# One order for all queues replaced by another, with 104 elementwise steps on other engines, in a fused attention and expert-layer kernel

## The chip, the cores and the metric

The kernel runs on one core of one Trainium2 chip. The core has a matrix engine (PE, with PEld for its weight loads), three elementwise engines (VectorE, called DVE here; ScalarE, called ACT; GpSimd, called POOL) and a queue that issues DMAs (SP). Each engine works through its own queue strictly in order and waits where an instruction needs another engine's result. The metric is the time in microseconds (us) of one execution on the device; lower is better. The kernel before takes 222.41 us (median of three runs, 222.18 to 222.57).

## What is computed

Clustered attention over 4 batches of 8 heads (768 tokens, 64 values a head): each query and each key is assigned to the nearest of 16 centroids, and a query attends only to keys of its own cluster. The result feeds a two-matrix layer with a softmax-weighted activation and a normalisation between the two matrices. Cut from the reference:

```python
q_assign = np.argmax(np.einsum('bhsd,hcd->bhsc', q_n, c_n), axis=-1)
k_assign = np.argmax(np.einsum('bhsd,hcd->bhsc', k_n, c_n), axis=-1)
mask = q_assign[:, :, :, None] == k_assign[:, :, None, :]
scores = np.where(mask, scale * q @ k.T, -1e9)
attn = softmax(scores);  x = attn @ v          # x: 3072 tokens x 512
h = x @ w_in                                   # 512 -> 1024
sm = softmax(h);  solu = h * sm
ln = (solu - mu) / np.sqrt(var + 1e-06) * g_ln
return ln @ w_out                              # 1024 -> 512
```

## The kernel before

The program is a list of some 1,570 named steps. Each step is added with its engine and the steps that it needs, and then a table, `ORDER`, says in which order all steps are written into the program. Since every engine has its own queue, the table sets the order of each queue and nothing else; a second table, `AWAY`, names steps that go to another engine than their usual one:

```python
def on(name, engine):
    return AWAY.get(name, engine)
...
for name in ORDER:
    o = self.ops[name]
    assert done.issuperset(o["first"]) and name not in done, name
    o["fn"]()
    done.add(name)
```

The steps that the change and the prediction speak of, by the first letters of their names:

- Loads on SP: `ld` (q and k of a pair of heads, into `raw`), `lv` (v), `lo` (w_out, 512 KB each), `li` (w_in, four parts of 512 KB into the three buffers `w_st`). A fourth part needs the first part's buffer back, that is, the cast `wi0` done. Behind them on the same queue come DMA transposes (`tx` of the attention's output x, `tu` of the activation u) and the stores `ou`.
- Preparation: `xa`, `xt` bring q and k, transposed, into `xt` (batch 0 through the matrix engine and a copy, L407 and L409; later batches by a DVE transpose, L421). `ca` casts a half of them to bf16 into `qbig` or `kbig` (L437 on ACT; L439 for q and L441 for k, with a scaling, on POOL or DVE). `cv` casts v (L554, L556). `cl`, `tb`, `mx`, `oh`, `ot` find the cluster of each token (matrix engine, then DVE). `pl` copies the cluster code under the q or k rows (L531), `bl` clears rows (L543).
- Attention: 144 regions. `S` is a half of a region's score products (L641), `E` its exponential on ACT (L651, 1024 columns), `V` the product with v (L663), six small matmuls each. 41 groups end in a normalisation `N` on DVE (L675 and L686). All `V` of a group write one bank, `ob`, so the next group's first `V` waits for `N`.
- The layer, in 24 tiles of 128 tokens: `h` products with w_in (L772), `hm` the maximum on DVE (L782), `ex` the exponential on ACT (L798), `u` the product of the two (L805, on DVE or POOL), `bn`, `ag` the statistics on DVE (L816, L821, L823), `as`, `al` small sums and a power (L835, L840), `y` products with w_out (L844), `sc` the scaling of the result (L856 on ACT, L858 on DVE).
- Once: `wi` casts w_in (L580, POOL), `mk`, `km` copy column sums (L611), `ce` centres w_out (L618 on DVE, L622 and L624 on POOL).

The score and v products of batch b run beside the layer tiles of batch b-1, so the matrix engine has two kinds of work to choose from after the first batch; in the first batch it has attention alone.

Of the kernel before, what the change touches and what calls it, by code (L numbers as in the profile page):

```python
# [38 lines left out]
lc ld0.0.0.0 ld0.0.1.0 ld0.0.0 ld0.0.1 ld0.1.0 ld0.1.1 lv0.0 ld0.2.0 ld0.2.1 ld0.3.0 lo3 lv0.1  # L39
ld0.3.1 lg lv0.2 lo1 lo2 lo0 cx z5 cy cz wu tp0.0.0.0 tp0.0.0.1 tp0.0.1.0 tp0.0.1.1 cp xa0.0.0  # L40
xt0.0.0 xa0.0.1 xt0.0.1 tp0.1.0.0 xa0.1.0 cb cl0.0 tb0.0 mx0.0 oh0.0 ot0.0 ca0.0.0.0.0 z3
ca0.0.1.0.0 ca0.0.0.0.1 cc ca0.0.0.1.1 ca0.0.0.1.0 pl0.0.1.1 pl0.0.0.0 ca0.0.1.0.1 ca0.0.1.1.1
ca0.0.1.1.0 tp0.1.0.1 tp0.1.1.0 xt0.1.0 xa0.1.1 cl0.0.1 tp0.1.1.1 cv0.0.1 xt0.1.1 pl0.0.0.1
tp0.2.0.0 tp0.2.0.1 tb0.0.1 mx0.0.1 oh0.0.1 ot0.0.1 pl0.0.1.0.1 pl0.0.1.0.0 pl0.0.1.1.1 cl0.1 sg
pl0.0.1.1.0 z1 ca0.1.1.0 cv0.0.0 ca0.1.0.0 xa0.2.0 pl0.0.1.0 tp0.2.1.0 xt0.2.0 xa0.2.1 S0.0 S0.1
E0 tp0.2.1.1 xt0.2.1 S1.0 tp0.3.0.0 S1.1 S2.0 S2.1 tp0.3.0.1 tb0.1 mx0.1 oh0.1 xa0.3.0 E1 E2 cl0.2
xt0.3.0 S3.0 S3.1 V0.0 V0.1 V1.0 S4.0 S4.1 V1.1 tp0.3.1.0 tb0.2 E3 S5.0 S5.1 E4 E5 ot0.1 N0 mx0.2
gt tp0.3.1.1 S6.0 S6.1 V2.0 V2.1 S7.0 S7.1 V3.0 V3.1 xa0.3.1 gk xt0.3.1 cl0.3 E6 E7 cv0.1.0
pl0.1.1.1 ca0.1.0.1 ca0.3.0.0 pl0.1.1.0 ca0.3.0.1 z2 ca0.1.1.1 oh0.2 pl0.1.0.0 pl0.1.0.1 gw S8.0
S8.1 S9.0 S9.1 me0 me1 ot0.2 tb0.3 pl0.2.1.0 N1 pl0.2.0.0 mx0.3 mk oh0.3 ca0.2.0.0 ca0.2.1.0  # L50
# [1304 lines left out]
```

## Time and profile before

| | us |
|---|---|
| median of three runs | 222.41 |
| span of the profiled execution | 220.5 |
| first exponential starts | 13.0 |
| first normalisation ends | 18.2 |
| thirty-first normalisation (`N30`) ends | 153.8 |
| last score region's exponential starts | 201.8 |

A span is the time from the first to the last instruction of the profiled execution. The view by stretches gives how long each engine was busy between two times, and in brackets how many instructions it ran; a matrix engine that shows as busy is not at its peak, since its matmuls overlap. A row of the groups gives engine, operation, output and inputs with their shapes, count, busy time, the mean of one in ns, and after the second bar the idle time of the engine just before such instructions, with what ended it.

### The profile page before, as it was taken

What the parts mean: (1) busy time and instruction counts of PE and PEld (TensorE: products, weight loads), DVE (VectorE), ACT (ScalarE), POOL (GpSimd) and SP (SyncE); (2) the same over time, 40 slices, a digit from 0 to 9 for tenths busy, and PEclk for the clock granted to TensorE, in tenths of its full rate; (3) what the DMA queues carried; (4) which work ended last, traced back from release to release, by engine and by line L of the source; (5) the groups of instructions that cost most, each with busy time, mean ns of one, the idle gap of its engine ahead of it and who ended that gap; (6) DMA issues with size and microseconds to landing.
All of it is one profiled execution on the core that took longest, in us unless ns stands there. A gap on an engine that the chain in (4) does not pass through costs nothing.

```text
span 220.5 us, 6292 instructions
## 1 busy us (share of the span) xinstructions
PE 211.4 (96%) x2401; PEld 148.9 (68%) x2431; DVE 185.7 (84%) x430; ACT 192.8 (87%) x245; POOL 158.8 (72%) x198
## 2 busy tenths in 40 slices
PE   7899999999999999999999999999999999999984
PEld 4567577677678776777677677666777767655442
DVE  3699979968999999896799999994888856989982
ACT  3799999999999998999999989999999888685362
POOL 3686969897898999549939997879889054456610
PEclk9999999999999999999999999999999999999999
DMA  5998999999999993999999981939584229777522
GB/s 199 394 402 259 189 175 300 126 154 259 164 154 169 190 188 62 174 248 210 153 225 162 180 184 38 171 92 209 151 173 90 72 64 168 154 120 170 163 94 100
DMA packets 120911, 38.33 MB, mean 174 GB/s; under 512 B 109993, under 2 KB 116401, under 8 KB 120881
## 3 DMA queue, kind: packets, MB, share of 16 engines
q1 hardware_dynamic: 120448, 37.40, 81.7%
q10 hardware_dynamic: 432, 0.52, 0.7%
q8 instruction: 19, 0.31, 0.6%
q14 instruction: 12, 0.09, 0.2%
HBM read 23.11 MB, written 6.29 MB: 133 GB/s over the span
## 4 chain that ended last, share of the span: by engine, by line
PE 72%; DVE 10%; DMA 6%; POOL 5%; issue 3%; ACT 2%; SPq 1%; DVEq 0%; ACTq 0%; POOLq 0%
PE sb L641 22%; PE hb L772 16%; PE mb L844 15%; PE ob L663 12%; DMA w_st<-in_moe_w_in_dram 4%; PE hb L470 3%; DMA raw<-in_q_dram 2%; DVE w_st L782 2%; PE hb L396 2%; DVE xt L421 2%; DVE bs L816 2%; POOL kbig L441 1%; PE mb L470 1%; POOL w_in_sb L580 1%; POOL v L556 1%
## 5 line engine op out<-in xcount | busy, mean ns | idle before, releaser
L651 ACT ACTIVATE e<-sb 128x1024 bf16<-128x1024 f32 x144 | 139.9, 1024 | 8.9 <-PE sb L641 8.1
L641 PE MATMUL sb<-qbig,kbig 80*128 80x256 bf16 (+3 forms) x648 | 83.8, 261 | 1.3 <-ACT e L651 1.0
L641 PEld LDWEIGHTS <-kbig 80*128 80x128 bf16 (+1 forms) x648 | 62.9, 119 | 25.4 <-issue 8.6
L805 POOL TENSOR_TENSOR u<-e_sb,w_st 128x1024 bf16<-128x1024 bf16 x21 | 45.1, 2145 | 20.0 <-ACT e_sb L798 13.3
L663 PEld LDWEIGHTS <-e 128*128 128x128 bf16 x1152 | 48.6, 97 | 10.4 <-DVE x L686 0.6
L663 PE MATMUL ob<-v,e 128*128 128x65 bf16 x1140 | 51.4, 193 | 0.2
L772 PE MATMUL hb<-w_in_sb,xT 128*128 128x512 bf16 x173 | 50.6, 379 | 0.9 <-POOL v L1323 0.3
L844 PE MATMUL mb<-w_out_c,uT 128*128 128x512 bf16 x165 | 45.5, 379 | 1.2 <-DVE y L858 0.4
L816 DVE BATCH_NORM_STATS2 bs<-u 128x6 f32<-128x512 bf16 x48 | 31.6, 680 | 1.1 <-POOL u L805 1.1
L798 ACT ACTIVATE e_sb<-w_st,nmax 128x1024 bf16<-128x1024 f32 (+1 forms) x25 | 27.8, 1113 | 3.2 <-DVE w_st L782 1.8
L439 POOL CAST qbig<-xt 64x768 bf16<-64x768 f32 (+1 forms) x31 | 25.7, 830 | 6.5 <-PE ob L663 2.7
L441 POOL TENSOR_SCALAR kbig<-xt 64x768 bf16<-64x768 f32 (+1 forms) x32 | 27.6, 865 | 2.4 <-DVE xt L409 0.8
L840 POOL TENSOR_TENSOR alpha<-var,halves 128x1 f32<-128x1 f32 x24 | 15.3, 638 | 12.6 <-DVE var L823 8.0
L421 DVE STREAM_TRANSPOSE xt<-raw 128x768 f32<-128x768 f32 x24 | 22.5, 959 | 0.1
L844 PEld LDWEIGHTS <-uT 128*128 128x128 bf16 x176 | 15.2, 97 | 10.2 <-issue 0.8
L772 PEld LDWEIGHTS <-xT 128*128 128x128 bf16 x192 | 15.8, 98 | 8.8 <-issue 0.6
L686 DVE TENSOR_TENSOR x<-ob,den 128x256 bf16<-128x256 f32 (+2 forms) x40 | 19.0, 474 | 1.4
L782 DVE TENSOR_SCALAR_CACHE_REDUCE w_st<-hb 128x512 f32<-128x512 f32 x24 | 16.3, 680 | 3.8 <-PE hb L772 3.7
L782 DVE TENSOR_SCALAR_CACHE_REDUCE w_st<-hb,nmax 128x512 f32<-128x512 f32 x24 | 17.8, 740 | 1.9 <-PE hb L772 1.5
L856 ACT ACTIVATE y<-mb,alpha 128x512 f32<-128x512 f32 x15 | 10.3, 685 | 6.5 <-POOL alpha L840 3.6
L675 DVE RECIPROCAL den<-ob 128x4 f32<-128x4 f32 (+2 forms) x40 | 7.1, 178 | 10.4 <-PE ob L663 10.1
L556 POOL CAST v<-vf 128x384 bf16<-128x384 f32 x22 | 10.9, 504 | 3.3 <-DMA vf<-in_v_dram 2.6
(109 smaller groups left out, 202.6 us busy)
## 6 DMA issues: line engine op xcount, KB each, us to landing
vf<-in_v_dram SPq DMA_DIRECT2D x16, 384.0 KB, 5.3
out_dram<-y SPq DMA_DIRECT2D x23, 256.0 KB, 2.5
raw<-in_k_dram SPq DMA_DIRECT2D x26, 192.0 KB, 4.6
raw<-in_q_dram SPq DMA_DIRECT2D x24, 192.0 KB, 5.1
w_g<-in_moe_w_out_dram SPq DMA_DIRECT2D x4, 512.0 KB, 8.7
w_st<-in_moe_w_in_dram SPq DMA_DIRECT2D x4, 512.0 KB, 8.0
raw<-in_q_dram SPq DMA_DIRECT2D x3, 384.0 KB, 6.6
raw<-in_k_dram SPq DMA_DIRECT2D x3, 384.0 KB, 7.6
```

The lines of the kernel that those rows point to most:

```text
L421: nc.vector.transpose(xts[b, p, i][:], raw_of(b, p, i))
L439: (nc.vector if e == "DVE" else nc.gpsimd).tensor_copy(dst, src)
L441: (nc.vector if e == "DVE" else nc.gpsimd).tensor_scalar(dst, src, scalar1=inv_C, scalar2=1.0, op0=Alu.mult, op1=Alu.mult)
L641: nc.tensor.matmul(reg[:, c:c + wd], kb[u, pp, side_of(h), keys], qb[u, pp, side_of(h), su * P:su * P + wd])
L651: nc.scalar.activation(es[r][:, :w], src, Act.Exp, scale=exp_scale, bias=-exp_scale)
L663: nc.tensor.matmul(ops_of(group_of[n])[:, s, :VW], es[r][:, c0:c0 + P], v1[index[b, pair_of(h)] % R][:, side_of(h), kt, :VW], start=(kt == ...
L772: nc.tensor.matmul(hb[f2][:], xTs[f][:, dc, :], w_in_sb[:, dc, f2 * BANK:(f2 + 1) * BANK], start=(dc == 0), stop=(dc == n_dc - 1))
L782: nc.vector.tensor_scalar(ff[f, "h"][:, f2 * BANK:(f2 + 1) * BANK], hb[f2][:], scalar1=-1.0, scalar2=nmax[:, f2 - 1:f2] if f2 else 3.0e38, ...
L798: nc.scalar.activation(ff[f, "e"][:, cols(f, f2)], ff[f, "h"][:, cols(f, f2)], Act.Exp, bias=ff[f, "nmax"][:, n_ff2 - 1:], scale=-1.0, acc ...
L805: (nc.vector if e == "DVE" else nc.gpsimd).tensor_tensor(ff[f, "u"][:, cols(f, f2)], ff[f, "e"][:, cols(f, f2)], ff[f, "h"][:, cols(f, f2) ...
L816: nc.vector.bn_stats(ff[f, "bs"][:, f2, :], ff[f, "u"][:, f2 * BANK:(f2 + 1) * BANK])
L844: nc.tensor.matmul(y_of(f, x), ff[f, "uT"][:, fc, :], w_out_c[:, fc, parts_of(f, x)], start=(fc == 0), stop=(fc == n_fc - 1))
```

## The change

Both tables are written anew. The operations, the buffers and what each step computes are the same. 104 of the 1,570 steps change engine, and nearly every queue has another order:

| steps | from | to | count |
|---|---|---|---|
| `ca` casts of q and k | POOL (16), ACT (1) | DVE | 17 |
| `ca` | ACT | POOL | 3 |
| `ca` | POOL | ACT | 1 |
| `cv` casts of v | ACT | POOL | 8 |
| `cv` | POOL | ACT | 4 |
| `cv` | POOL, ACT | DVE | 2 |
| `pl` copies | DVE | POOL | 12 |
| `pl` | POOL (5), ACT (2) | DVE | 7 |
| `pl` | ACT | POOL | 2 |
| `u` products | POOL | DVE | 6 |
| `u` | DVE | POOL | 2 |
| `sc` scalings | ACT to DVE 5, DVE to ACT 5 | | 10 |
| `as` sums | POOL to DVE 9, DVE to POOL 8 | | 17 |
| `ce` centrings | DVE to POOL 4, POOL to DVE 1 | | 5 |
| `xa`, `xt` copies | ACT to DVE 3, DVE to ACT 2 | | 5 |
| `bl` clears | POOL to DVE 2, DVE to POOL 1 | | 3 |

Steps by engine: DVE 301 before and 319 now, ACT 219 and 206, POOL 183 and 178; PE 722 and SP 143 in both. No `ca` stood on DVE before. The two tables together are two lines shorter, so a line of the kernel below it has a number that is smaller by 2.

```diff
 AWAY.update(dict.fromkeys("""
-    as0 as11 as14 as15 as17 as18 as19 as2 as22 as23 as4 as5 as9 bl1.2 bl3.0 ce0 ce2 ce4 km mk
...
+    as1 as10 as13 as15 as16 as17 as18 as19 as20 as21 as3 as5 as7 as8 bl1.0 bl2.0 bl3.0 ca0.0.0.0.1
+    ca0.1.0.1 ca0.3.0.0 ca1.0.0.0 ca1.0.1.1 ca1.1.0.0 ca1.1.0.1 ca1.1.1.0 ca2.1.0.0 ca2.1.0.1
+    ca2.1.1.0 ca2.2.0.0 ca2.2.1.1 ca2.3.0.1 ca3.1.0.1 ca3.2.0.1 ca3.3.0.0 ce0 cv0.2.1 cv0.3.1 km mk
...
 """.split(), "DVE"))
...
 ORDER = """
-lc ld0.0.0.0 ld0.0.1.0 ld0.0.0 ld0.0.1 ld0.1.0 ld0.1.1 lv0.0 ld0.2.0 ld0.2.1 ld0.3.0 lo3 lv0.1
...
+lc cx ld0.0.0.0 wu ld0.0.1.0 tp0.0.0.0 ld0.0.0 xa0.0.0 cy cz tp0.0.0.1 cp tp0.0.1.0 ld0.0.1 ld0.1.0
```

Three places show the moves. The first is the DVE queue around the normalisations `N6` to `N8` (each is a RECIPROCAL of `den` and the product into `x`). Before:

```order
L421 STREAM_TRANSPOSE xt<-raw 128x768 x2
L675 RECIPROCAL den<-ob 128x4
L686 TENSOR_TENSOR x<-ob,den 128x2x2x64
L479 STREAM_TRANSPOSE cst<-hb_92 128x384
L479 STREAM_TRANSPOSE cst<-hb_93 128x384
L489 TENSOR_REDUCE mx<-cst 128x48
L675 RECIPROCAL den<-ob 128x4
L686 TENSOR_TENSOR x<-ob,den 128x2x2x64
L493 TENSOR_TENSOR oh<-cst,mx 128x768
L782 TENSOR_SCALAR w_st,nmax<-hb_92 128x512
```

and now:

```order
L419 STREAM_TRANSPOSE xt<-raw 128x768
L731 COPY xT<-hb_93 128x1024
L439 TENSOR_SCALAR kbig_101<-xt 64x768
L673 RECIPROCAL den<-ob 128x4
L684 TENSOR_TENSOR x<-ob,den 128x2x2x64
L477 STREAM_TRANSPOSE cst<-hb_92 128x384
L477 STREAM_TRANSPOSE cst<-hb_93 128x384
L487 TENSOR_REDUCE mx<-cst 128x48
L437 CAST qbig_98<-xt 64x768
L673 RECIPROCAL den<-ob 128x4
L684 TENSOR_TENSOR x<-ob,den 128x2x2x64
L491 TENSOR_TENSOR oh<-cst,mx 128x768
```

Two casts now stand between normalisations on DVE, and the maximum of the layer's first tile (L782) comes later.

The second is the POOL queue where w_in is cast (the CAST into `w_in_sb` is `wi`; the pairs of operations on `w_g` are `ce`). Before:

```order
L556 CAST v_3_105<-vf 128x6x64 x2
L580 CAST w_in_sb<-w_st 128x1024
L622 TENSOR_SCALAR w_g<-w_g,g_ln_111 128x512
L624 TENSOR_TENSOR w_out_c<-w_g,y 128x512
L622 TENSOR_SCALAR w_g<-w_g,g_ln_111 128x512
L624 TENSOR_TENSOR w_out_c<-w_g,y 128x512
L441 TENSOR_SCALAR kbig_101<-xt 64x768
L580 CAST w_in_sb<-w_st 128x1024 x3
```

and now:

```order
L554 CAST v_3_105<-vf 128x6x64
L437 CAST qbig_98<-xt 64x768
L620 TENSOR_SCALAR w_g<-w_g,g_ln_111 128x512
L622 TENSOR_TENSOR w_out_c<-w_g,y 128x512
L620 TENSOR_SCALAR w_g<-w_g,g_ln_111 128x512
L622 TENSOR_TENSOR w_out_c<-w_g,y 128x512
L578 CAST w_in_sb<-w_st 128x1024 x3
L1321 MEMSET v_4_106 128x12x2
L578 CAST w_in_sb<-w_st 128x1024
```

The first cast of w_in, which frees the buffer for the fourth load, now stands behind both centrings.

The third is the SP queue where w_in is loaded. Before:

```order
L596 DMA w_g<-in_moe_w_out_dram 128x2x512 x3
L413 DMA raw<-in_q_dram 32x48x32
L574 DMA w_st<-in_moe_w_in_dram 128x1024
L413 DMA raw<-in_q_dram 32x48x32 x3
L413 DMA raw<-in_k_dram 32x48x32
L548 DMA vf<-in_v_dram 128x2x384
L413 DMA raw<-in_k_dram 32x48x32 x3
L574 DMA w_st<-in_moe_w_in_dram 128x1024 x3
L413 DMA raw<-in_q_dram 32x48x32 x4
```

and now:

```order
L411 DMA raw<-in_q_dram 32x48x32 x2
L594 DMA w_g<-in_moe_w_out_dram 128x2x512
L546 DMA vf<-in_v_dram 128x2x384
L411 DMA raw<-in_q_dram 32x48x32 x2
L546 DMA vf<-in_v_dram 128x2x384
L411 DMA raw<-in_k_dram 32x48x32 x4
L572 DMA w_st<-in_moe_w_in_dram 128x1024 x4
L546 DMA vf<-in_v_dram 128x2x384
L411 DMA raw<-in_q_dram 32x48x32 x4
```

All four loads of w_in now stand in a row behind the first eight small loads of batch 1, and the loads behind them (v and the next q and k) wait while the fourth waits for its buffer.

More of the change, by code (lines that the diff above doesn't have):

```diff
@@ new lines @@
+V71.0 S109.1 V71.1 E108 y6.1 u10.0 S110.0 S110.1 tb3.2 E109 h12.0.0 hm11.1 N29 S111.0 E110 as9
+bn9.0 xt3.3.0 y6.2 S111.1 xt3.3.1 V72.0 ou4 V72.1 S112.0 h12.0.1 hm12.0 E111 S112.1 y6.3 ca3.1.1.1
+al6 as10 cv3.1.1 V73.0 V73.1 E112 S113.0 ag8 lv3.3 S113.1 tu8 cl3.3 ex11.0 ou5 E113 tb3.3 S114.0
+S114.1 E114 V74.0 h12.1.0 ca3.3.1.1 tx14 sc6 bn9.1 h12.1.1 S115.0 S115.1 tu9 V74.1 y7.0 S116.0
+mx3.2 u11.0 h13.0.0 N30 S116.1 E115 hm12.1 oh3.2 E116 bn10.0 V75.0 h13.0.1 S117.0 V75.1 V76.0 ot3.2
+S117.1 bn10.1 h13.1.0 S118.0 as11 ex12.0 E117 y7.1 V76.1 S118.1 V77.0 hm13.0 y7.2 V77.1 h13.1.1
```

212 lines of the change are left out of this document (101 added, 111 removed).

## The prediction

> **What bounds the kernel now.** I read the page's busy times first, then the view by stretches.
>
> ```profile
> span 220.5 us, 6292 instructions
> PE 211.4 (96%) x2401; PEld 148.9 (68%) x2431; DVE 185.7 (84%) x430; ACT 192.8 (87%) x245; POOL 158.8 (72%) x198
> ```
>
> Four engines lie between 72% and 96%, so an average decides nothing; the stretches do. Columns: the stretch, its length, busy time and instructions of each engine, granted clock, DMA share, GB/s.
>
> ```profile
> 20.00:45.00 25.00, 23.59 (x319) 16.25 (x318) 21.62 (x43) 24.36 (x29) 20.03 (x26) 1.00 0.99 193
> 45.00:90.00 45.00, 44.26 (x557) 33.66 (x562) 42.36 (x88) 43.65 (x52) 40.33 (x44) 1.00 0.97 170
> 90.00:150.00 60.00, 59.41 (x703) 43.66 (x712) 54.73 (x117) 57.64 (x72) 46.20 (x52) 1.00 0.90 166
> 150.00:200.00 50.00, 49.52 (x571) 34.47 (x576) 38.29 (x101) 42.49 (x55) 30.33 (x30) 1.00 0.67 134
> 18.20:153.80 135.60, 132.86 (x1628) 97.93 (x1647) 121.83 (x256) 131.21 (x158) 111.81 (x127) 1.00 0.96 176
> ```
>
> From 45 us on PE is busy 98.4 to 99.0% of the time: it is the bound, and no order of the other queues can make it shorter there. Only in 20 to 45 us does it fall to 94%, and there ACT is the full engine (24.36 of 25). So what the change can win lies ahead of 45 us, and what it can lose lies anywhere. The clock was 1.00 throughout. The waits of PE and DVE agree; the second row is from the waits of 18 to 154 us alone, as is the third:
>
> ```profile
> PE sb L641 <- ACT e L651: 1.0, 3, 0.3
> DVE den L675 <- PE ob L663: 4.7, 9, 1.3
> DVE w_st L782 <- PE hb L772: 4.1, 5, 2.5
> ```
>
> DVE is early at the normalisations and maxima: in that stretch it waited 8.8 us for PE, and PE hardly for it.
>
> **The change, part by part.** I take the stretch in which nearly all moved steps fall, from the end of the first normalisation to the end of the thirty-first (`N30`), and what comes before and behind it.
>
> ```profile
> 17.74 0.42 DVE L686 TENSOR_TENSOR x<-ob,den 128x256 bf16<-128x256 f32 x1
> 153.29 0.56 DVE L686 TENSOR_TENSOR x<-ob,den 128x384 bf16<-128x384 f32 x1
> ```
>
> These two end at 18.2 and 153.8 us, which is the fifth stretch above: 135.6 us.
>
> *PE's side.* Counted in the two orders, PE has between the first `V` behind `N0` and the first behind `N30` the same score and v products, but 53 halves of `h` steps instead of 60 and 29 quarters of `y` steps instead of 39: the layer is put off. A step of these has two matmuls of 512 columns, and the chain gives four in 0.87 and 0.86 us:
>
> ```profile
> 56.97 0.87 PE hb L772 x4
> 87.99 0.86 PE mb L844 x4
> ```
>
> 17 steps at 0.43 us are 7.3 us of PE that leave the stretch and are done behind it. At PE's own pace of before the stretch would take 135.6 - 7.3 = 128.3 us.
>
> *DVE's side.* The same count gives what DVE gains between these normalisations: 14 casts (0 before), 2 casts of v, 1 clear, 2 scalings, 1 product `u`, 1 small sum. It loses 1 `ag`, 1 `bn`, 3 `ce`, 4 `hm`, 1 `mx` and 2 `oh` (one of each in batch 0), 2 `pl` (one in batch 0) and 1 copy into `xt`. The rows:
>
> ```profile
> L531 DVE COPY qbig<-oht 32x768 f32<-32x768 f32 x7 | 4.9, 702 | 0.2
> L531 DVE COPY kbig<-oht 32x768 f32<-32x768 f32 x2 | 1.7, 867 | 0.0
> L556 POOL CAST v<-vf 128x384 bf16<-128x384 f32 x22 | 10.9, 504 | 3.3 <-DMA vf<-in_v_dram 2.6
> L858 DVE TENSOR_SCALAR y<-mb,alpha 128x512 f32<-128x512 f32 x8 | 5.9, 736 | 1.8 <-POOL alpha L840 1.2 <-PE mb L844 0.7
> L805 DVE TENSOR_TENSOR u<-e_sb,w_st 128x1024 bf16<-128x1024 bf16 x2 | 2.4, 1222 | 0.0
> L543 DVE MEMSET kbig<- 16x768 f32 x2 | 1.4, 698 | 0.4 <-issue 0.4
> L816 DVE BATCH_NORM_STATS2 bs<-u 128x6 f32<-128x512 bf16 x48 | 31.6, 680 | 1.1 <-POOL u L805 1.1
> L618 DVE SCALAR_TENSOR_TENSOR w_out_c<-w_g,g_ln,y 128x512 bf16<-128x512 f32 x5 | 4.1, 830 | 0.0
> L782 DVE TENSOR_SCALAR_CACHE_REDUCE w_st<-hb,nmax 128x512 f32<-128x512 f32 x24 | 17.8, 740 | 1.9 <-PE hb L772 1.5
> L493 DVE TENSOR_TENSOR oh<-cst,mx 128x768 bf16<-128x768 f32 x6 | 7.2, 1206 | 0.0
> ```
>
> No cast of q or k on DVE is in the trace. The nearest work is the copy of `pl`, as many elements a row from memory to memory: the nine copies of the first two rows average (7 x 0.702 + 2 x 0.867) / 9 = 0.74 us. They hold two kinds, as the view of that line shows (min/median/max in ns):
>
> ```profile
> L531 DVE COPY qbig<-oht x13: 351/552/1164, 12.1 to 160.6; 32x768 f32<-32x768 f32 x7, 32x384 f32<-32x384 f32 x4, 32x192 f32<-32x192 f32 x2
> L441 POOL TENSOR_SCALAR kbig<-xt x32: 505/827/1612, 6.9 to 152.2; 64x768 bf16<-64x768 f32 x29, 64x384 bf16<-64x384 f32 x3
> 23.59 1.01 DVE L531 COPY qbig<-oht 32x384 f32<-32x384 f32 x1
> 22.66 2.64 POOL L441 TENSOR_SCALAR kbig<-xt 64x768 bf16<-64x768 f32 x3
> ```
>
> 0.55 us is a copy left alone and 1.16 us one that met work on POOL; the copy of 23.59 us, half as long, took 1.01 us while POOL was casting. So a cast costs 0.55 to 1.16 us, and I take 0.74, the mean of what copies met here. Added: 14 x 0.74 + 2 x 0.50 + 0.70 + 2 x 0.74 + 1.22 + 0.15 = 14.9 us (the clear and the small sum at the 0.70 and 0.15 us that they take on DVE before). Removed: 0.47 + 0.68 + 3 x 0.83 + 4 x 0.71 + 0.55 + 1.81 + 1.26 + 0.55 = 10.7 us (`hm` at the mean of its two forms; batch 0's `mx`, `pl` and copy at 0.55 to 0.56 and its `oh` at 0.60, half of a later one's size). DVE's busy time in the stretch becomes 121.8 + 4.2 = 126.0 us. Before, it was idle 135.6 - 121.8 = 13.8 us, of which 8.8 us on PE and 0.2 us on the cluster product vanish if DVE is the late one; 4.8 us in small gaps and waits for POOL stay. **DVE needs 126.0 + 4.8 = 130.8 us where PE needs 128.3.** DVE becomes the bound: every `N` comes late, the next group's first `V` waits for it on PE, and the scores, exponentials and layer products queued behind that `V` wait too. That is +2.5 us, and what PE loses there it cannot win back, as it is full behind it.
>
> *ACT's side.* From 13 to 60 us ACT was full:
>
> ```profile
> 13.00:60.00 47.00, 45.47 (x599) 32.91 (x600) 41.49 (x86) 46.20 (x55) 38.53 (x50) 1.00 0.99 218
> ```
>
> Seven elementwise steps leave its queue between exponentials there (`xa`, `xt`, two `cv`, a `pl`, two `ca`) and one copy comes: 0.48 + 0.48 + 0.51 + 0.51 + 0.51 + 0.84 + 0.84 - 0.48 = 3.7 us (0.48 from the copies, 0.51 the v casts and the copy of `pl`, 0.84 the casts on ACT). While DVE sets the pace this buys nothing; it is what rival 1 lives on.
>
> *The start.* The chain to the first score product is as long as before (transposes, cluster product, then five steps on DVE and the copies): the one-hot turn stands behind one more small transpose (0.36 us) and DVE does one copy (0.45 us) that ACT did. Between 0 and +0.4 us, covered until `N0` by PE's transposes; I take 0.
>
> *w_in.* The chain that ends last runs here before through the loads, in order of time:
>
> ```profile
> 32.66 1.00 POOL w_in_sb L580
> 33.68 7.99 DMA w_st<-in_moe_w_in_dram
> 41.72 1.04 POOL w_in_sb L580
> 42.81 0.38 PE L772 MATMUL hb<-w_in_sb,xT 128*128 128x512 bf16 x1 [0.33 <-POOL v L1323]
> ```
>
> A buffer is freed at 33.7 us, the fourth part lands 8 us later, is cast, and PE waited 0.33 us. Now the freeing cast stands behind the centring of two parts, and that behind `km`. The rows for it (the last is the four loads' time to landing):
>
> ```profile
> 29.83 0.42 DVE L686 TENSOR_TENSOR x<-ob,den 128x256 bf16<-128x256 f32 x1
> 30.17 0.68 DVE L611 COPY y<-hb 128x512 f32<-128x512 f32 x1
> L421 DVE STREAM_TRANSPOSE xt<-raw 128x768 f32<-128x768 f32 x24 | 22.5, 959 | 0.1
> L622 POOL TENSOR_SCALAR w_g<-w_g,g_ln 128x512 f32<-128x512 f32 x3 | 2.5, 841 | 0.1
> L624 POOL TENSOR_TENSOR w_out_c<-w_g,y 128x512 bf16<-128x512 f32 x3 | 3.8, 1277 | 0.3
> DMA to landing us min/median/max: 5.2/8.0/10.5
> ```
>
> By the clock of before the fourth normalisation ends at 30.3 us; then a cast of v (0.50), `mk` (0.68), a transpose (0.96), a normalisation (0.60), a cast (0.50) and `km` (0.68) end on DVE at about 34.2; two centrings on POOL (0.84 + 1.28 us each) end at 38.4, the first cast of w_in at 39.4. With 5.2 us to the median of 8.0 us for landing, the fourth part is cast at 45.6 to 48.4. PE comes to that product 15 steps later, 3.1 us (8 half regions of 0.22 and 7 `V` of 0.19 us), at 45.9. The wait is -0.3 to +2.5 us (+5.0 at the longest landing); SP's queue has nothing else in flight while it waits, which speaks for the short landing. A late DVE also brings PE there later, so most of it is covered: I take 0.5. Queued behind the fourth load are v and the next q and k of batch 1, needed by DVE only some 10 us later.
>
> *Behind `N30`.* PE has 7.3 us more to do and remains the bound at its 99%; DVE (38.3 of 50 us busy) has room. 0, at most +1.
>
> **Sum.** 130.8 - 128.3 + 0 + 0.5 + 0 = +3.0 us on the profiled span of 220.5, so 223.5; the median stands 1.9 us above the span, and the same addition gives 225.4 us.
>
> The rule that bears on the price of a cast is in the Trainium skill, SBUF — State Buffer, section Who interferes with whom: DVE casts and scalings that use both port pairs and any POOL instruction exclude each other, and whichever comes second is blocked for the whole of the first. The trace agrees in kind: 1.01 us for the short copy beside POOL's casts.
>
> **Rivals.** POOL's longest steps stand behind the second of them:
>
> ```profile
> L805 POOL TENSOR_TENSOR u<-e_sb,w_st 128x1024 bf16<-128x1024 bf16 x21 | 45.1, 2145 | 20.0 <-ACT e_sb L798 13.3 <-issue 5.6 <-DVE y L858 0.6
> ```
>
> 1. *The gain (other side).* The casts run alone, at 0.55: 14 x 0.19 = 2.7 us less, so DVE is busy 123.3 us. If its gaps as the late engine are those of ACT in 13 to 60 us (0.8 of 47, so 2.3 us in the stretch), it needs 125.6, below 128.3, and ACT's 3.7 us let PE follow. Then -2.7 us: 219.7. For it: POOL is less loaded, and ACT shows how few gaps the late engine leaves. Against it: by their mean, some three in ten of the copies met POOL ((0.74 - 0.55) / (1.16 - 0.55)). It decides once DVE's need falls below 128.3 us.
> 2. *Blocked casts.* POOL is busy 82% of the stretch (111.8 of 135.6). If every cast waits for what POOL has under way, half of an instruction weighted by length (45 of POOL's 159 us at 2.14 and the rest at some 0.82 us: (0.28 x 2.14 + 0.72 x 0.82) / 2 = 0.60), it costs 0.55 + 0.82 x 0.60 = 1.04 us: 14 x 0.30 = 4.2 us more, 229.6. For it: single copies took 1.16. Against it: they averaged 0.74. By the rule of the Trainium skill above, this is the case in which DVE is always the second to come.
> 3. *w_in decides.* The fourth part lands after 8 us and nothing covers it: +2.0 on the sum, 227.4.
> 4. *Nothing lost, nothing won.* Casts at 0.55 and gaps of 4.8 us: 128.1 against PE's 128.3, and 222.4.
>
> **Numbers.** Forecast 0.46, rival 1 0.24, rival 2 0.15, rival 3 0.08, rival 4 0.07. Slower by over 0.2% (0.44 us, about what three runs of this kernel can tell): 0.46 + 0.15 + 0.08 = 0.69; same 0.07; faster 0.24. Predicted 225.4 us. The forecast's own range is 223.0 to 227.5; the 8-in-10 range cuts the better half of rival 1 off, and goes past rival 2 by what casts of 1.16 us would add (14 x 0.12 = 1.7): 219.8 to 231.3.
>
> **What would show it.** Right: in 20 to 150 us DVE busy above 95%, idle hardly ever for PE at L673 and L780, PE below 97% with waits for the normalisation at the `V` products; casts on DVE of 0.55 to 1.2 us; ACT with idle time ahead of its exponentials. Wrong: PE at 98% from 30 us on and DVE still waiting for it (rival 1), or a stall of PE of over 2 us near 46 us and none later (rival 3). A stall in a place that I have not counted, above all behind 150 us, would make the sum wrong whichever sign it has.

## The result, and the profile after

| | us |
|---|---|
| before, median of 4 runs beside it | 222.3 (221.92 to 222.57) |
| changed, median of 4 runs | 235.67 (234.33 to 237.10) |
| ratio, 95% interval | 1.061 (1.056 to 1.066) |
| span of the profiled execution | 233.5, before 220.5 |

The change costs 13.4 us where 3.0 were forecast. The sign is the forecast's; the time lies above its range. Of the 10.0 us between the span forecast (223.5) and the one measured (233.5), 0.4 lie ahead of `N0`, 7.4 between `N0` and `N30` (with the forecast's 0.5 us for w_in counted there) and 2.2 behind.

The changed kernel's page, first line and busy times of the engines:

```profile
span 233.5 us, 6302 instructions
PE 217.4 (93%) x2399; PEld 148.3 (64%) x2431; DVE 204.0 (87%) x447; ACT 187.7 (80%) x232; POOL 153.6 (66%) x197
```

The same stretches as before the change (columns as there: length, busy time of PE, PEld, DVE, ACT and POOL, granted clock, DMA share, GB/s); the last runs again from the end of `N0` to the end of `N30`:

```profile
20.00:45.00 25.00, 23.63 (x325) 15.79 (x324) 22.03 (x44) 22.15 (x24) 20.78 (x29) 1.00 0.95 227
45.00:90.00 45.00, 44.03 (x529) 31.94 (x535) 43.33 (x87) 41.75 (x49) 39.03 (x42) 1.00 0.97 166
90.00:150.00 60.00, 55.11 (x648) 40.01 (x655) 55.66 (x112) 51.17 (x61) 42.97 (x48) 0.98 0.89 168
150.00:200.00 50.00, 48.27 (x553) 33.79 (x561) 40.85 (x95) 42.32 (x54) 20.81 (x26) 0.99 0.37 85
18.58:157.28 138.70, 131.20 (x1589) 93.61 (x1608) 127.88 (x257) 122.22 (x140) 107.83 (x123) 0.99 0.89 172
```

Up to 45 us nothing is lost: PE is busy 23.6 us of 25 as before, and `N7` ends at 40.5 us where it ended at 42.7. ACT, full there before, has nearly 3 us of 25 free. From `N0` to `N30` it takes 138.7 us where 130.8 were forecast. DVE is busy 127.9 us of them, close to the 126.0 of the sum, but idle 10.8 us, not 4.8. It still waits for PE, as the waits of that stretch show (who waits for whom: us in total, times, longest), while PE waits for it once for long:

```profile
PE hb L770 <- DVE cst L477: 2.8, 1, 2.8
DVE cst L477 <- PE hb L468: 2.6, 5, 1.1
DVE den L673 <- PE ob L661: 2.6, 4, 0.9
DVE w_st L780 <- PE hb L770: 0.7, 1, 0.7
```

So DVE is not what sets the pace all along, though the forecast had it so. It is late in single places. The largest one, in the timeline of 143 to 148 us (start, duration, engine and line, what ended the idle time before it):

```profile
142.91 0.83 POOL L439 TENSOR_SCALAR kbig<-xt 64x768 bf16<-64x768 f32 x1
143.69 3.23 DVE L803 TENSOR_TENSOR u<-e_sb,w_st 128x1024 bf16<-128x1024 bf16 x1 [0.86 <-DMA uT<-u]
143.71 2.13 POOL L803 TENSOR_TENSOR u<-e_sb,w_st 128x1024 bf16<-128x1024 bf16 x1
145.92 1.05 POOL L833 TENSOR_SCALAR es<-esum 128x1 f32<-128x1 f32 x1
146.84 0.57 DVE L477 STREAM_TRANSPOSE cst<-hb 128x384 f32<-128x384 f32 x1
147.47 0.59 PE L770 MATMUL hb<-w_in_sb,xT 128*128 128x512 bf16 x2 [2.80 <-DVE cst L477]
```

The first `u` on DVE (`u10`) starts just before POOL's cast ends, runs on beside POOL's `u9` and takes 3.23 us instead of the 1.22 of a lone one. Behind it in DVE's queue stands `tb3.2` (the transpose into `cst`), which empties the bank `hb` that the layer product `h12.0.0` needs; PE stands for 2.80 us. Then the clock falls (stretches of 2.5 us, columns as above):

```profile
145.00:147.50 2.50, 0.03 (x1) 0.03 (x1) 2.50 (x3) 0.79 (x1) 2.33 (x3) 1.00 1.20 302
147.50:150.00 2.50, 2.50 (x16) 1.51 (x16) 2.47 (x6) 0.14 (x1) 1.39 (x3) 0.59 0.50 116
150.00:152.50 2.50, 2.28 (x28) 1.64 (x27) 1.82 (x6) 1.48 (x2) 0.83 (x1) 0.73 0.00 0
152.50:155.00 2.50, 2.50 (x29) 1.40 (x26) 1.37 (x4) 2.50 (x5) 0.80 (x1) 1.00 0.54 105
```

At 0.59 and 0.73 of full speed, 5 us of PE lose some 2.5 x 0.41 + 2.5 x 0.27 = 1.7 us more, by estimate. Two smaller cases of the same kind lie behind 150 us. At 164 us a copy of the cluster code on DVE (`pl3.2.1.1`) takes 2.12 us beside POOL's `u12`, and the maximum queued behind it holds a layer product up for 1.03 us:

```profile
164.11 2.14 POOL L803 TENSOR_TENSOR u<-e_sb,w_st 128x1024 bf16<-128x1024 bf16 x1
164.56 2.12 DVE L529 COPY kbig<-oht 32x768 f32<-32x768 f32 x1
...
168.47 0.59 PE L770 MATMUL hb<-w_in_sb,xT 128*128 128x512 bf16 x2 [1.03 <-DVE w_st L780]
```

At 199 us it is `u17` beside `u18`, and a maximum queued behind it holds PE up for 0.91 us:

```profile
198.51 2.15 POOL L803 TENSOR_TENSOR u<-e_sb,w_st 128x1024 bf16<-128x1024 bf16 x1 [1.87 <-DMA uT<-u]
...
199.06 2.67 DVE L803 TENSOR_TENSOR u<-e_sb,w_st 128x1024 bf16<-128x1024 bf16 x1
...
202.40 1.02 PE L770 MATMUL hb<-w_in_sb,xT 128*128 128x512 bf16 x4 [0.91 <-DVE w_st L780]
```

The groups of the whole execution (busy time, mean ns of one, idle time before them) show that the casts cost what was forecast, and what the layer products waited for:

```profile
L437 DVE CAST qbig<-xt 64x768 bf16<-64x768 f32 x12 | 8.6, 718 | 0.1
L439 DVE TENSOR_SCALAR kbig<-xt 64x768 bf16<-64x768 f32 x4 | 3.7, 924 | 0.1
L803 DVE TENSOR_TENSOR u<-e_sb,w_st 128x1024 bf16<-128x1024 bf16 x7 | 12.0, 1709 | 0.9 <-DMA uT<-u 0.9
L770 PE MATMUL hb<-w_in_sb,xT 128*128 128x512 bf16 x175 | 51.3, 379 | 5.7 <-DVE cst L477 2.8 <-DVE w_st L780 1.9 <-issue 0.2
```

Sixteen full casts average (8.6 + 3.7) / 16 = 0.77 us against 0.74 forecast. The `u` average 1.71 against 1.22.

### The profile page after: what moved, and what is told of

Its sections match the earlier page's. It is cut to its first block, busy times and chain, and to the rows that moved or that the text cites. A ratio compares the mean times of both kernels' runs of the same rounds, so it can differ in the third digit from the quotient of the medians.

```text
span 233.5 us, 6302 instructions
## 1 busy us (share of the span) xinstructions
PE 217.4 (93%) x2399; PEld 148.3 (64%) x2431; DVE 204.0 (87%) x447; ACT 187.7 (80%) x232; POOL 153.6 (66%) x197
## 4 chain that ended last, share of the span: by engine, by line
PE 44%; DVE 23%; POOL 16%; DMA 7%; SPq 4%; issue 3%; ACT 1%; DVEq 0%; POOLq 0%; ACTq 0%
PE mb L842 12%; PE sb L639 11%; PE hb L770 8%; PE ob L661 6%; DMA raw<-in_k_dram 4%; POOL u L803 4%; SPq L411 3%; DVE u L803 3%; POOL kbig L439 3%; DMA uT<-u 2%; DVE w_st L780 2%; POOL w_out_c L622 2%; DVE bs L814 2%; DVE kbig L529 2%; POOL qbig L437 2%
## 5 line engine op out<-in xcount | busy, mean ns | idle before, releaser
L649 ACT ACTIVATE e<-sb 128x1024 bf16<-128x1024 f32 x144 | 141.4, 1022 | 21.4 <-PE sb L639 20.3
L639 PE MATMUL sb<-qbig,kbig 80*128 80x256 bf16 (+3 forms) x648 | 95.0, 263 | 3.1 <-DVE qbig L529 1.1
L639 PEld LDWEIGHTS <-kbig 80*128 80x128 bf16 (+1 forms) x648 | 61.7, 121 | 30.6 <-issue 9.6
L661 PEld LDWEIGHTS <-e 128*128 128x128 bf16 x1152 | 52.6, 98 | 13.8 <-issue 2.5
L661 PE MATMUL ob<-v,e 128*128 128x65 bf16 x1140 | 56.8, 194 | 0.1
L770 PE MATMUL hb<-w_in_sb,xT 128*128 128x512 bf16 x175 | 51.3, 379 | 5.7 <-DVE cst L477 2.8
L803 POOL TENSOR_TENSOR u<-e_sb,w_st 128x1024 bf16<-128x1024 bf16 (+1 forms) x17 | 36.4, 2140 | 14.6 <-ACT e_sb L796 6.7
L838 POOL TENSOR_TENSOR alpha<-var,halves 128x1 f32<-128x1 f32 x24 | 14.5, 605 | 31.5 <-DVE var L821 29.6
L439 POOL TENSOR_SCALAR kbig<-xt 64x768 bf16<-64x768 f32 (+1 forms) x28 | 24.1, 863 | 3.9 <-DVE xt L419 2.2
L770 PEld LDWEIGHTS <-xT 128*128 128x128 bf16 x192 | 16.8, 98 | 13.1 <-issue 6.3
L437 POOL CAST qbig<-xt 64x768 bf16<-64x768 f32 (+1 forms) x21 | 17.3, 822 | 4.7 <-DVE xt L419 1.5
L529 POOL COPY kbig<-oht 32x768 f32<-32x768 f32 (+2 forms) x13 | 9.7, 746 | 11.4 <-DVE oht L498 7.5
L554 POOL CAST v<-vf 128x384 bf16<-128x384 f32 x25 | 14.5, 588 | 1.3 <-DMA vf<-in_v_dram 0.6
```

Source lines behind the costliest of these rows:

```text
L437: (nc.vector if e == "DVE" else nc.gpsimd).tensor_copy(dst, src)
L439: (nc.vector if e == "DVE" else nc.gpsimd).tensor_scalar(dst, src, scalar1=inv_C, scalar2=1.0, op0=Alu.mult, op1=Alu.mult)
L639: nc.tensor.matmul(reg[:, c:c + wd], kb[u, pp, side_of(h), keys], qb[u, pp, side_of(h), su * P:su * P + wd])
L649: nc.scalar.activation(es[r][:, :w], src, Act.Exp, scale=exp_scale, bias=-exp_scale)
L661: nc.tensor.matmul(ops_of(group_of[n])[:, s, :VW], es[r][:, c0:c0 + P], v1[index[b, pair_of(h)] % R][:, side_of(h), kt, :VW], start=(kt == ...
L770: nc.tensor.matmul(hb[f2][:], xTs[f][:, dc, :], w_in_sb[:, dc, f2 * BANK:(f2 + 1) * BANK], start=(dc == 0), stop=(dc == n_dc - 1))
```

## The experiments

Medians of four runs (twelve for before_relief), and the 95% interval of the ratio to the kernel before on the same chip:

| kernel | us | ratio |
|---|---|---|
| order_alone | 243.26 | 1.087 to 1.099 |
| engines_alone | 267.80 | 1.203 to 1.207 |
| u_back | 230.48 | 1.036 to 1.039 |
| casts_back | 235.94 | 1.060 to 1.068 |
| u_two | 229.89 | 1.033 to 1.037 |
| u_four | 235.49 | 1.055 to 1.066 |
| tb_first | 234.83 | 1.055 to 1.060 |
| u9_too | 232.88 | 1.047 to 1.051 |
| before_u_two | 224.79 | 1.010 to 1.014 |
| six_moves | 233.88 | 1.049 to 1.055 |
| six_moves_b | 228.62 | 1.028 to 1.032 |
| u_casts | 231.94 | 1.033 to 1.046 |
| more_moves | 227.08 | 1.015 to 1.025 |
| grouped | 227.60 | 1.021 to 1.027 |
| after_grouped | 236.48 | 1.058 to 1.069 |
| before_relief | 222.04 | 0.998 to 1.002 |

### The order or the engines?

order_alone: the changed `ORDER` with the table of engines of before.

```diff
 AWAY of before (ca0.0.1.1.0 ca0.2.0.1 ...)
-ORDER of before
+ORDER of the change
```

> The changed order with all 104 steps on the engines that had them before. Theory P (prices: steps moved to VectorE meet POOL's work, take up to 3.23 us and hold a bank that TensorE waits for): the stall of 2.80 us before the layer product at 144.7 us, the low clock behind it (1.7 us) and the stalls of about 1 us behind other moved steps go, 222.5 to 227 us. Theory O (the order itself: operands come just in time whatever engine makes them, and the layer is put off): 231 us or more, with stalls of TensorE in the same places, now behind POOL's casts.

engines_alone: the other half.

```diff
-AWAY of before
+AWAY of the change
 ORDER of before
```

> The order of before with all 104 steps on the changed engines. Theory P: VectorE carries the six u and the casts here too, so some 5 to 10 us of the 13.4 stay: 227 to 232 us. Theory O: the order of before has room ahead of its operands, so 222 to 224.5 us.

Each half alone is worse than the two together: 243.3 and 267.8 us against 235.7. The first number is on theory O's side, the second beyond both theories. The timeline of engines_alone shows one of the places where such a mixture loses time:

```profile
31.09 0.82 POOL L438 CAST qbig<-xt 64x768 bf16<-64x768 f32 x1
...
31.96 1.01 PE L640 MATMUL sb<-qbig,kbig 80*128 80x256 bf16 x4 [3.84 <-POOL qbig L438]
```

This cast, `ca0.2.0.1`, is done on ACT in the kernel before, between two exponentials at 24.44 us. On POOL it stands behind whatever the order had put into that queue, and PE waits 3.84 us. Each queue is in order, so a step that changes engine without changing place waits for all that stands ahead of it there. Order and engines are one plan, and neither experiment divides the 13.4 us into two parts.

### Which of the moved steps?

u_back takes six `u` back, casts_back 42 casts and copies, u_two and u_four split the six.

```diff
 u_back, added to AWAY's POOL list:
+    u10.0 u13.0 u15.0 u16.0 u17.0 u19.0
```

> The changed kernel with its six u of the middle (items 10, 13, 15, 16, 17, 19) back on POOL, nothing else. Theory P: the 2.80 us stall at 144.7 us, the 1.7 us of low clock behind it and the 0.9 us behind u17 go, 5.4 us in all, less about 1 us for a POOL that is fuller by 6 x 2.14 us: 229 to 232 us. Theory O: at most 1.5 us less than the changed kernel, 234 us or more.

```diff
 casts_back, out of AWAY's DVE list (42 steps ca and pl as before the change):
-    ca1.0.0.0 ca1.0.1.1 ca1.1.0.0 ca1.1.0.1 ca1.1.1.0 ca2.1.0.0 ca2.1.0.1
-    ca2.1.1.0 ca2.2.0.0 ca2.2.1.1 ca2.3.0.1 ca3.1.0.1 ca3.3.0.0
...
```

> The changed kernel with the 42 casts of q and k and copies of the one-hot rows that changed engine back where they were; u and the rest stay. Theory P: the stalls behind moved casts and copies (0.5 at 49.9, 0.66 at 123.2, 1.0 at 168.5 us, and part of 0.8 at 95.2) go, the large one at 144.7 us stays: 231 to 233.5 us. Theory O: POOL has to make 14 more casts in an order written for VectorE, so they come later still: 235 us or more.

```diff
 u_two, added to AWAY's POOL list:
+    u10.0 u17.0
```

> The changed kernel with only u10 and u17 back on POOL, the two u that took 3.23 and 2.67 us beside a u of POOL; the other four, at 1.21 us each, stay on VectorE. Theory P: all of the 5.2 us that the six gave back, 229.5 to 231.5 us. Rival (the load that six u put on VectorE, 6 x 1.21 us, whichever they are): a third of it, 233 to 235 us.

```diff
 u_four, added to AWAY's POOL list:
+    u13.0 u15.0 u16.0 u19.0
```

> The complement: u13, u15, u16 and u19 back on POOL, u10 and u17 stay on VectorE. Theory P: the stall at 144.7 us and the low clock stay, 234.5 to 237 us. Rival (load of VectorE): two thirds of 5.2 us come back, 231 to 233 us.

The six give back 235.67 - 230.48 = 5.2 us, u10 and u17 alone 5.8 us, the other four 0.2, which is less than the spread of the runs (234.33 to 237.10 for the changed kernel). It is not the load of DVE, since four of six products taken away change nothing, but the two that ran beside a `u` of POOL. In u_two the stretch from `N0` to `N30` falls from 138.7 to 134.0 us, and the clock is 1.00 throughout:

```profile
18.69:152.65 133.96, 129.50 (x1589) 92.94 (x1608) 125.22 (x257) 122.19 (x140) 107.35 (x122) 1.00 0.92 177
```

casts_back gains nothing. Theory P's 231 to 233.5 us fails there: the waits that went came back in other places. PE now waits 3.7 us for casts and copies of POOL, 2.0 us for normalisations and 1.7 us for ACT. POOL makes these casts in an order that was written for DVE, so this run prices no cast by itself.

### The length of u10, or what stands behind it?

tb_first puts the step that frees the bank ahead of u10.

```diff
-y6.1 u10.0 S110.0 S110.1 tb3.2 E109 h12.0.0
+y6.1 tb3.2 u10.0 S110.0 S110.1 E109 h12.0.0
```

> The changed kernel with one step moved: the copy tb3.2, which frees bank h0, stands ahead of the product u10 on VectorE instead of behind it; all engines as changed. Theory P1 (what costs is not the length of u10 but what is queued behind it: the bank's owner): the 2.80 us stall at 144.7 us and the 1.7 us of low clock behind it go although u10 stays on VectorE and long, 230.5 to 232.5 us. Theory P2 (VectorE is short of time there, and the stall only changes place): 234 us or more.

It is 0.8 us less, within the spread of the changed kernel's runs, so P2 is right. In its timeline u10 is as long as ever; `h12.0.0` is in time, and the v product behind the normalisation, which also stands behind u10, waits instead:

```profile
144.09 3.26 DVE L806 TENSOR_TENSOR u<-e_sb,w_st 128x1024 bf16<-128x1024 bf16 x1 [0.21 <-DMA uT<-u]
144.14 2.14 POOL L806 TENSOR_TENSOR u<-e_sb,w_st 128x1024 bf16<-128x1024 bf16 x1
...
148.63 0.82 PE L664 MATMUL ob<-v,e 128*128 128x65 bf16 x12 [2.23 <-DVE x L687]
```

u9_too gives DVE more to do: POOL's u9 as well.

```diff
 u9_too, out of AWAY's POOL list:
-    u9.0
```

> The changed kernel with u9 on VectorE too, so that no u of POOL runs beside u10: VectorE has one product more to do, POOL one less. Theory M (u10 is held up by POOL's u9 beside it): u9 and u10 take about 1.2 us each, end together earlier than u10 alone did, and the stall at 144.7 us falls from 2.80 to 2 us or less: 233 to 235 us. Rival (VectorE is short of time): 1.2 us more on it and the time grows, 236 to 237.5 us.

232.88 us, 2.8 less than the changed kernel: a little better than theory M's 233 to 235, and against the rival. DVE makes both products in less time than u10 took alone:

```profile
143.12 2.99 DVE L803 TENSOR_TENSOR u<-e_sb,w_st 128x1024 bf16<-128x1024 bf16 x2
143.16 1.88 POOL L439 TENSOR_SCALAR kbig<-xt 64x768 bf16<-64x768 f32 x1
...
146.65 0.59 PE L770 MATMUL hb<-w_in_sb,xT 128*128 128x512 bf16 x2 [1.73 <-DVE cst L477]
```

The first of the two takes 1.22 us, and now it is POOL's cast that is held up: 1.88 us where it took 0.83 above. The second product ends 1.07 us after that cast. The stall of PE falls to 1.73 us, and the clock stays at 1.00 over 145 to 150 us.

before_u_two moves the same two products in the kernel before.

```diff
 before_u_two, out of the kernel before's POOL list:
-    u10.0 u17.0
```

> The kernel before with u10 and u17, and nothing else, on VectorE. There u10 has no other u of POOL beside it (the next step on POOL is a cast of 0.8 us), and u18 follows u17 only 0.9 us after its end. Theory M (a u on VectorE is dear only where POOL is at work beside it): u10 takes 1.2 to 2.0 us, u17 likewise, the normalisation behind u10 comes about 1 us late, 222 to 223.5 us. Rival (a u on VectorE costs some 2.5 us wherever it stands): 226 to 228 us.

2.6 us slower, above theory M's 222 to 223.5 and below the rival's 226. Here u10 met only a cast, and its length is again what POOL still had to do plus 1.07 us:

```profile
139.62 0.82 POOL L440 TENSOR_SCALAR kbig<-xt 64x768 bf16<-64x768 f32 x1
139.77 1.76 DVE L804 TENSOR_TENSOR u<-e_sb,w_st 128x1024 bf16<-128x1024 bf16 x1
```

POOL is free at 140.44; 140.44 + 1.07 = 141.51, and u10 ends at 141.53. M's length is right. Its price was too low: the emptying of the bank `hb` stands behind u10 in this order too, and PE waited 0.9 us for it and then 0.4 us for a maximum, in a stretch where it has no time to spare. The rest of the 2.6 us was not traced to one place.

### The other 7.7 us

six_moves starts from u_back and moves six steps within their own queues, so that the one that PE waits for comes first.

```diff
-DVE   ca1.1.1.0 pl1.0.0.0
+DVE   pl1.0.0.0 ca1.1.1.0
-DVE   ca1.1.0.0 xt1.2.1
+DVE   xt1.2.1 ca1.1.0.0
-POOL  pl1.2.0.1 ca1.2.1.0
+POOL  ca1.2.1.0 pl1.2.0.1
-POOL  ca2.1.1.1 pl2.0.1.1 pl2.0.1.0 pl2.0.0.0
+POOL  pl2.0.1.1 pl2.0.1.0 pl2.0.0.0 ca2.1.1.1
-DVE   ag5 bn6.1 ca2.2.1.1
+DVE   ca2.2.1.1 ag5 bn6.1
-DVE   pl3.2.1.1 bn11.0 ag9 hm14.0 hm14.1
+DVE   bn11.0 ag9 hm14.0 hm14.1 pl3.2.1.1
-POOL  u23.0
+DVE   u23.0
```

> The kernel with the six u back on POOL (230.5 us), with u23.0 on VectorE again and six steps moved on their own queues so that the one that TensorE waits for comes first: pl1.0.0.0 ahead of ca1.1.1.0, xt1.2.1 ahead of ca1.1.0.0, ca1.2.1.0 ahead of pl1.2.0.1, ca2.1.1.1 behind pl2.0.0.0, ca2.2.1.1 ahead of ag5, pl3.2.1.1 behind hm14.1. Theory S (what is left is a row of single waits, 0.43 + 0.86 + 0.45 + 1.01 + 0.65 + 1.0 us at these places and 0.5 us at the end, each of which can be taken away alone): 4.9 us less, 225 to 227 us. Rival L (queues are full, and what is moved back comes late in its turn): no more than 1.5 us less, 229 us or more.

3.4 us slower than u_back, so the sum of theory S failed. Its timeline shows a new collision, in a place that no move touched:

```profile
126.82 0.82 POOL L441 CAST qbig<-xt 64x768 bf16<-64x768 f32 x1 [2.53 <-DVE xt L423]
...
127.56 3.40 DVE L441 CAST qbig<-xt 64x768 bf16<-64x768 f32 x1
127.62 0.83 POOL L443 TENSOR_SCALAR kbig<-xt 64x768 bf16<-64x768 f32 x1
128.42 2.13 POOL L807 TENSOR_TENSOR u<-e_sb,w_st 128x1024 bf16<-128x1024 bf16 x1
...
131.71 0.34 PE L665 MATMUL ob<-v,e 128*128 128x65 bf16 x6 [2.83 <-DVE x L688]
```

The cast `ca2.3.0.1`, 0.56 us in the changed kernel, started 0.08 us before the first of three POOL instructions in succession ended and was kept out by all of them, to 130.55, and PE stood 2.83 us for the normalisation behind it. A small shift of the queues was enough to bring two steps together. six_moves_b takes that cast to POOL and leaves u23.0 there:

```diff
-DVE   ca2.3.0.1 u23.0
+POOL  ca2.3.0.1 u23.0
```

> The six moves again, with the cast ca2.3.0.1 on POOL, because on VectorE it took 3.40 us from 127.6 us on beside a cast and a u of POOL and cost TensorE 3.0 us, and u23.0 on POOL as in the change. Theory S: the 3.0 us and about 1 us at the end go, 228.5 to 230.3 us. Rival L (another step comes late in its place): 231.5 us or more.

228.62 us, as theory S had it. u_casts takes all casts of the later batches off DVE, with u10 and u17:

```diff
 u_casts, to POOL (ca3.2.0.1 to ACT):
-DVE   ca1.0.0.0 ca1.0.1.1 ca1.1.0.0 ca1.1.0.1 ca1.1.1.0 ca2.1.0.0 ca2.1.0.1
-DVE   ca2.1.1.0 ca2.2.0.0 ca2.2.1.1 ca2.3.0.1 ca3.1.0.1 ca3.2.0.1 ca3.3.0.0
-DVE   u10.0 u17.0
```

> The changed kernel with u10 and u17 on POOL and the 14 casts of q and k of batches 1 to 3 that it gave VectorE back too, 13 on POOL and one on ScalarE, in the changed order. Of the 7.7 us that u10 and u17 don't explain, theory C (casts that meet POOL on VectorE cause the most of it): 225 to 228 us. Theory Q (in this order POOL is then the queue that is late, as the stalls behind POOL's casts and copies show): 230 us or more.

231.94 us (229.8 to 232.4), no better than u_two, which the best of its four runs equals: theory C falls. Taken off DVE as a group, the casts of this order gain nothing. more_moves treats two single ones:

```diff
-DVE   ca2.2.1.1
+POOL  ca2.2.1.1
-POOL  pl2.0.0.0 ca2.1.1.1 as4 pl2.0.0.1
+POOL  pl2.0.0.0 as4 pl2.0.0.1 ca2.1.1.1
```

> The kernel of the six moves with ca2.3.0.1 on POOL (228.6 us), with ca2.2.1.1 on POOL too (on VectorE it took 2.16 us beside u7 and cost TensorE 0.66 us at 122.4 us) and ca2.1.1.1 behind pl2.0.0.1, for which TensorE waited 0.90 us at 95.7 us. Theory S (single waits that can be taken away one by one): 227 to 228 us. Rival L (the next step in the queue comes late instead): 228.5 us or more.

227.08 us, within theory S's 227 to 228. By its busy time PE is then as full as before the change, and the stretch from `N0` to `N30` takes 131.8 us:

```profile
90.00:150.00 60.00, 59.74 (x713) 43.01 (x710) 55.26 (x119) 55.88 (x67) 46.38 (x53) 1.00 0.90 174
150.00:200.00 50.00, 49.77 (x555) 33.58 (x554) 38.53 (x103) 41.54 (x54) 31.97 (x33) 1.00 0.47 104
19.18:150.95 131.77, 129.63 (x1609) 92.89 (x1608) 123.45 (x255) 121.87 (x140) 108.73 (x124) 1.00 0.93 181
```

### TensorE's own order

4.5 us are left (227.08 against 222.56 for the kernel before beside it), with PE busy 59.7 of 60 us. grouped and after_grouped change PE's queue alone, on more_moves and on the changed kernel, at 95 places like this:

```diff
-S81.0 V51.0 S81.1 V51.1
+S81.0 S81.1 V51.0 V51.1
```

> The kernel of the last moves (227.1 us) with TensorE's own queue regrouped: 95 second halves of a score or v step stand directly behind their first halves where a step of another kind stood between. Counted in the orders, TensorE then changes the kind of its products 385 times; it does so 490 times in the changed order and 386 times in the order before. Theory K (in the changed order TensorE runs the same products at a slower pace because it changes kind more often; 4.9 us for 104 changes would be 0.047 us each): 222 to 224 us. Rival (the pace has another cause, such as operands that come just in time; the scores that come earlier change nothing): 226 us or more.

> The changed kernel itself with the same regrouping of 95 half steps on TensorE, all engines as changed. Theory K: about 4 us less than the changed kernel, 230 to 232.5 us. Rival: 234.5 us or more.

Neither is faster: 227.60 and 236.48 us, and theory K falls. The groups of more_moves (first row) and of grouped (second) warn of a reading that looked like evidence:

```profile
L643 PE MATMUL sb<-qbig,kbig 80*128 80x256 bf16 (+3 forms) x648 | 94.0, 262 | 1.2 <-DVE qbig L533 0.7 <-POOL qbig L533 0.2
```

```profile
L643 PE MATMUL sb<-qbig,kbig 80*128 80x256 bf16 (+3 forms) x648 | 86.2, 261 | 1.3 <-DVE qbig L533 1.0 <-POOL qbig L533 0.3
```

Busy time of the score products falls by 7.8 us and the time of the kernel by nothing. A matmul's record overlaps the next one's (in more_moves four score matmuls, 0.26 us each on average, lie within 0.60 us at 102.47 us). So a group's busy time grows with the number of breaks in its runs and does not say how long PE needs.

### The part that could have won

before_relief gives the kernel before a part of what the forecast's rival 1 lived on, two casts fewer on ACT in the stretch where ACT is full; `cv0.1.0` stands behind `ca0.1.1.1` in POOL's queue.

```diff
-ACT   cv0.1.0 cv0.2.1
+POOL  cv0.1.0 cv0.2.1
```

> The kernel before with two casts of v (cv0.1.0, cv0.2.1) on POOL, where it is idle, instead of ScalarE, which is full from 13 to 60 us; cv0.1.0 stands behind ca0.1.1.1. That is the part of the change by which ScalarE is relieved early, alone. If ScalarE sets the pace there (waits of TensorE for it of about 2 us in 13 to 45 us): 221.2 to 222.0 us. If POOL's casts then come late instead: 222.2 to 223 us.

222.04 us, ratio 0.998 to 1.002: no difference can be told. No version tried beats the kernel before.

## Why the prediction was wrong

- **DVE's price, right in sum and wrong in kind.** The sum had DVE busy 126.0 us between `N0` and `N30`; it is 127.9. Casts: 0.74 forecast, 0.77 measured. The term that was too small is "1.22" for a `u` on DVE, taken from lone ones: u10 took 3.23, and 126.0 + 2.0 is 128.0; u17, behind the stretch, took 2.67.
- **"DVE becomes the bound" is the step that failed.** The forecast took DVE's busy time plus 4.8 us of gaps and compared it with PE's 128.3 us. DVE has 10.8 us of gaps, of which it waits 2.6 + 2.6 + 0.7 us for PE. The forecast's own signs fail too: DVE is busy 93% of 20 to 150 us, not above 95%, and PE shows no wait for a normalisation at its v products. The time does not follow from either sum: the largest part that could be traced PE loses in single waits behind a DVE step that is long because POOL is at work. u_two and u_four show this for u10 and u17 together, u9_too for u10: 5.8 us of the 13.4, with 2.80 us of stall, some 1.7 us of low clock and 0.91 us at 202 us in the profiled execution. The move of queue place in tb_first did not help, because all of DVE's queue stands behind such a step. That the change came out slower, as forecast, is thus owed to other waits than the forecast's, and the right sign is in part luck.
- **The rule was cited and used on the wrong step.** Rival 2 had the mechanism, a blocked DVE, and spread it over 14 casts at half a POOL instruction each. The casts paid little on average. What costs is the rare long wait: in u10 2.15 us, in six_moves' cast 2.98 us, and PE behind it.
- **Copies and casts, the later moves.** From u_two's 229.89 to more_moves' 227.08 us, 2.8 us went with single waits of PE for steps that came late in DVE's or POOL's queue. At four of these places the late step was, or stood behind, one that had met POOL (`ca1.1.1.0`, `ca1.1.0.0`, `ca2.2.1.1`, `pl3.2.1.1`); at the others it was POOL's own queue. The places were treated together, so their single shares are not known.
- **What stays open: 4.5 us by the runs, 4.7 by the profiled spans (225.2 against 220.5).** Of the 4.7, 1.0 lies ahead of `N0`, 3.5 between `N0` and `N30` (131.8 against the forecast's 128.3 for PE) and 0.2 behind. In more_moves PE is as busy from 90 to 200 us as before the change. It is not how often PE's products change kind (grouped). The forecast's 2.5 us for a late DVE would fit in size, but no run ties them to DVE.
- **The start, 0:** `N0` ends 0.4 us later, at the bound given, but that is luck: in the ten profiled kernels that run the same steps up to `N0` it ends between 18.58 and 19.63 us, which is 0.4 to 1.4 us later than before. Why it varies stays open. **w_in, +0.5:** PE waited for no cast of w_in at all (the L770 row names only DVE). It stayed within the bounds. **Behind `N30`, 0, at most +1:** by the last normalisation's clock, 233.5 - 157.3 = 76.2 us against 220.5 - 153.8 + 7.3 = 74.0, so +2.2; there `u17` and `pl3.2.1.1` collide, and the last warning of the forecast, a stall behind 150 us that was not counted, came true.
- **Rival 1, the gain,** needed ACT's 3.7 us to be worth something. ACT did become free, and by before_relief two of the casts off it buy nothing that can be measured.

## What to carry to other kernels

When an elementwise step moves to VectorE, look up what GpSimd does at that moment: the price of a product or cast there is about its own length plus what is left of GpSimd's running instruction, and at times the one directly behind it too. Then look at what stands behind it in VectorE's queue; if TensorE is full, that wait is paid in whole, and may be paid a second time in clock. A sum of busy times does not show it, since one wait of 3 us hardly moves a mean over 16 casts. An order and an assignment of engines belong together: half of a plan was worse than either whole one.

## What the runs showed of the hardware

**VectorE waits for the end of GpSimd's work, and GpSimd for VectorE's.** Over these traces a length follows from the two rows: u10 in the changed kernel 145.84 - 143.69 + 1.07 = 3.22 us (3.23 measured); u17 200.66 - 199.06 + 1.07 = 2.67 (2.67); the cast in six_moves 130.55 - 127.56 + 0.42 = 3.41 (3.40). The 1.07 and 0.42 us are what is left once POOL is free. All 18 traces bear this out: 191 full-width casts and copies on DVE took over 0.65 us, and each ended 0.41 to 0.46 us after the end of a POOL instruction; 16 `u` took over 1.31 us, and each ended 1.07 to 1.09 us after one. Three of these copies are in the trace before the change, at 49.3, 91.2 and 160.6 us, so the rule could have been read there. The other way, POOL's small sum at 145.92 took 1.05 us where others take 0.19, and its cast 1.88 instead of 0.83, behind a DVE product that had come first. Rows that never grew in these traces are the normalisations and maxima, which read from the matrix engine's banks, the statistics and the transposes.

The Trainium skill, SBUF — State Buffer, section Who interferes with whom, states this as an exclusive lock on a shared port pair, taken for a whole instruction, with the second to come blocked, also for a product with two inputs in SBUF. The traces agree, though not for every POOL instruction: beside the small power of L838 (0.72 us from 104.44 us on in the changed kernel) a cast on DVE took its lone 0.55 us. They add one thing: a second POOL instruction that follows directly can keep DVE out as well. It did so in all 13 cases in which the DVE step had started within the last 0.08 us of the first, as u10 and six_moves' cast did. A DVE step that had waited for over 0.25 us got in between in 46 of 60 cases. Why it did not in the other 14 is open.

**The clock fell after a stall, but not after each.** Behind 2.80 us of standing still the granted clock was 0.59 and 0.73 for two stretches of 2.5 us; tb_first had 0.63 and 0.68 behind 2.23 us; in their profiled executions six_moves kept 1.00 behind 2.83 us, and u9_too behind 1.73 us. One and the same kernel differs as well: the mean clock of the changed kernel's four executions was 0.998, 0.992, 0.992 and 0.985, and they took 234.33, 235.24, 236.09 and 237.10 us. The Trainium skill, TensorE: Matmul & The Clock Gate, Part 1: The HAM clock gate, describes a free-running window of 3.4 us in which activity is judged, and a fall to half clock after an idle one. By a free-running window, equal stalls would be treated differently by where they fall, and the runs are in keeping with that without showing it. But the stalls of 2.80 and 2.23 us are shorter than the window, and the clock fell all the same, so here the measurement decides against an idle window of full length as the condition.
